# A memory-recurrent attention step: a postponed turning moves between the halves of P times V, a quarter of a filler unit moves behind the output products

## The chip, the cores and the metric

The kernel runs on one core of a Trainium2 chip. The metric is the device time of one execution in microseconds (us); several executions are measured and their median is given. The engines are called by the names of the profile: PE (matrix products; PEld are its weight loads), DVE, ACT and POOL (vector work and copies), SP (issues transfers). Each engine works through its own queue in the order in which the program was written.

## The reference

One block of a transformer, forward and backward, in bfloat16: sequence length 2048, model width 448. Attention runs over 64 segments of 32 tokens, one after the other; each segment is preceded by 8 memory tokens, which are the first 8 outputs of the segment before.

```
for s in range(n_seg):                       # 64 segments
    xs = x[:, s*32:(s+1)*32, :]
    h = concatenate([mem, xs], axis=1)       # 8 + 32 = 40 tokens
    q, k, v = h @ Wq, h @ Wk, h @ Wv         # 16 heads of 256
    p = softmax(where(mask, q @ k^T * scale, -1e9))
    o = (p @ v) @ Wo
    mem = o[:, :8, :]
    outs.append(o[:, 8:, :])
h  = x + A(layernorm(x));  h2 = h + swiglu_ffn(layernorm(h))
```

The outputs are h2 and the gradients with respect to the input, the first memory and all weights.

## The kernel before

The program has four stages: the forward chain over the 64 segments, the feed-forward part with its gradients, the backward chain over the segments, and a tail with the weight gradients. The change touches only the first, `forward_chain`. The order on every engine there is the order of the code: no scheduler moves anything.

A step `s` of the loop is one segment; four steps make one tile of 128 tokens (`t = s // 4`, `r = s % 4`). The step computes only what depends on the memory. A segment's window of 32 tokens in `hA` holds the 8 memory tokens and the first 24 tokens of the segment. The last 8 tokens of each segment do not become memory's input; for four segments together they make 32 rows of their own (`hB`), whose projections and output products are done in units that are spread over the steps as filler.

**Filler units.** `cur` is the unit of this step, `late` that of the step before. At r = 0 the unit is `o_units(t - 1)`: the output products of those 32 rows of the tile before. At r = 1, 2, 3 it is `b_units(t + 1, ...)` for k, q and v of the next tile. A unit has the parts u1 (first half of its columns), e1 (its copy out), u2 and u3 (two quarters, into one accumulator `p1`), e3 (the copy of `p1`), and, in a later step, ut (turning: PE transposes the result) and et (the copies of what was turned). For k and q, ut is 8 transposes and et two copies on ACT; for v both are empty; for `o_units`, u2 and u3 are 16 products of 224 columns each, e3 a copy on ACT into `partB`, ut two float32 transposes and et four small sums on DVE.

**A step, in order.** K and Q of the window (`proj`, line 545, 64 products), their turning (line 559), V (line 553), scores (line 590), softmax on DVE and ACT, u1 of the filler, the turning of P in two halves (`p_turn`, line 863) with copies by ACT for half 0 and by DVE for half 1 (`p_ev`), and u2 between them. Then P times V (line 897) in two halves, each of which makes two accumulators `po` (four in all). Each `po` is emptied by two copies: a large one into `oA` right away (DVE for `gg` = 0, ACT for `gg` = 1) and a small one into `oB`, collected in the list `obs` and issued after both halves. Between the halves stands `cur["u3"]()`. Then the output products (`wo_mm`, line 674, 64 of 224 columns) go into the accumulator `pO`, in the order in which the parts of `oA` become ready. DVE copies `pO` into `part`; `turn(part)` (line 598, two float32 transposes) and two sums on DVE (`gsum`, line 603) make the next segment's memory tokens in `hA`, with which the next step's projections start. While DVE copies `pO`, PE does `late["ut"]()`, and at r = 0 `prep_pe` (line 529: four transposes of the next tile's rows). `prep_ev` copies those (four copies on ACT, one on DVE) and `prep_load` fetches the rows of the tile after that on SP's queue. et follows one step later, at the head of the step, through `late2`.

**Accumulators.** All of them but the two for the scores come from the pool `psA` (`ps1`, line 499) with six buffers of 128 x 512 float32. A new accumulator gets a buffer whose last use in the code lies before the allocation; its first product waits until that use has ended.

Copies in this stage go through the helpers `V` (DVE, line 505), `A` (ACT, line 508) and `G_` (POOL, line 511), so all copies of an engine have one line in the profile; their shapes tell them apart: 128x256 are the large copies of `po`, 128x64 the small ones, 128x224 the copy of `pO`.

Of the kernel before, what the change touches and what calls it, by code (L numbers as in the profile page):

```python
# [265 lines left out]
def run_all(k: _K):  # L266
# [115 lines left out]
    with tc.manual_schedule():  # L382
# [86 lines left out]
        feed = ffn_phase(k, WT, ff, ffn, mv2, rstd2, {"o": Wo2, "v": Wv2, "k": Wk2, "q": Wq2}, back)  # L469
        k.feed = feed  # L470
        forward_chain(k, hA, NWIN, Wq_sb, Wk_sb, Wv_sb, Wo_sb, maskr, fwd, fwd, ff, feed)
        nc.gpsimd.dma_start(out=memTd[0:DB], in_=memT_all[0:DB].rearrange("p c s m -> p c (s m)"))
        next(feed)
# [7 lines left out]
def forward_chain(k: _K, hA, NWIN, Wq_sb, Wk_sb, Wv_sb, Wo_sb, maskr, work, stage, ff, feed):  # L481
    nc, tc = k.nc, k.tc
    S, D, M, H, Dh, HD = k.S, k.D, k.M, k.H, k.Dh, k.HD
    SEG, L, NSEG, NT, KC, DP, MC, DC = k.SEG, k.L, k.NSEG, k.NT, k.KC, k.DP, k.MC, k.DC
# [14 lines left out]
    def ps1(dtype=FP32):  # L499
        if dtype == FP32:  # L500
            return k.pspool.tile([P, 512], FP32, tag="ps", name="psf")
        return k.pspool.tile([P, 1024], BF16, tag="ps", name="psh")

    def V(out, in_):
        nc.vector.tensor_copy(out=out, in_=in_)  # L505

    def A(out, in_):
        nc.scalar.copy(out=out, in_=in_)  # L508
# [4 lines left out]
    def slot(s):  # L513
        return s % NWIN
# [3 lines left out]
    def fw(kc):  # L518
        return (kc % 2) * 2 * DB + (kc // 2) * DB

    def prep_load(t):
        xl = work.tile([P, DP], BF16, name="xload", tag="xload", bufs=1)
        nc.sync.dma_start(out=xl[:, 0:D], in_=dr["XN"][t * P:(t + 1) * P, :])
        return xl

    def prep_pe(xl):
        pt = ps1(BF16)
        for kc in range(KC):
            nc.tensor.transpose(pt[0:DB, kc * P:(kc + 1) * P], xl[:, fw(kc):fw(kc) + DB], ident[:, :])
        return pt  # L530

    def prep_ev(pt, t):
        v = pt[0:DB, 0:KC * P].rearrange("p (c r j) -> p c r j", c=KC, r=4)
        s0 = slot(4 * t)
        for r in range(4):
            A(hA[0:DB, :, s0 + r, M:SEG], v[:, :, r, 0:XA])
        hB = stage.tile([P, KC, 4, M], BF16, name="hB", tag="hB", bufs=2)
        V(hB[0:DB], v[:, :, :, XA:SEG])
        return hB
# [55 lines left out]
    def turn(src):  # L595
        y = ps1(FP32)
        for j in range(2):
            nc.tensor.transpose(y[0:DB, j * P:(j + 1) * P], src[:, j * DB:(j + 1) * DB], identf[:, :])
        return y[0:DB, 0:2 * P].rearrange("p (c b n) -> p c n b", c=KC, b=2)
# [13 lines left out]
    tiles = {}  # L613
# [63 lines left out]
    def o_units(t):  # L677
        T = tiles[t]
        st = {}

        def mm(i0, i1):
            for i in range(i0, i1):
                for c in range(4 * i, 4 * i + 4):
                    wo_mm(st["pO"], T.oB[:, c, :], c, c % 2, c < 2, c >= MC - 2)

        def u1():
            st["pO"] = ps1(FP32)
            mm(0, 4)

        def e1():  # L690
            pass

        def u2():
            mm(4, 6)

        def u3():
            mm(6, 8)

        def e3():
            A(partB[:, 0:2 * DB], st["pO"][:, 0:2 * DB])  # L700

        def ut():
            st["y"] = turn(partB)

        def et():
            for kc in range(KC):
                gsum(T.aT[0:DB, kc, :].rearrange("p (r j) -> p r j", r=4)[:, :, XA:SEG],
                     st["y"][:, kc, :, :].rearrange("p (r i) g -> p r i g", r=4))
        return dict(u1=u1, e1=e1, u2=u2, u3=u3, e3=e3, ut=ut, et=et)

    def none_units():
        def f():
            pass
        return dict(u1=f, e1=f, u2=f, u3=f, e3=f, ut=f, et=f)
# [18 lines left out]
    def v_b_rows(s, V_sb):  # L733
        t, r = divmod(s, 4)
        for g in range(G):
            gg, g2 = divmod(g, 2)
            eng = nc.gpsimd if s == 0 else nc.sync
            eng.dma_start(out=V_sb[QB * gg + SEG:QB * gg + L, g2 * GF:(g2 + 1) * GF],
                          in_=tiles[t].vB[32 * g + M * r:32 * g + M * (r + 1), :])
# [11 lines left out]
    xl = k.xl0  # L751
    tiles[0].hB = prep_ev(prep_pe(xl), 0)
    xl_next = k.rest_rows()
# [13 lines left out]
    mask_mm(0)  # L767
    mask_mm(1)
    late = none_units()
    late2 = none_units()  # L770

    for s in range(NSEG):
        t, r = divmod(s, 4)
        sl = slot(s)
        T = tiles[t]
        if r == 0:
# [7 lines left out]
            cur = o_units(t - 1) if t > 0 else none_units()  # L784
        else:
            cur = b_units(t + 1, "?kqv"[r]) if t + 1 < NT else none_units()
# [1 line left out]
        def stat(kc):  # L788
            return hA[0:DB, kc, sl, :]

        late2["et"]()
        kT = work.tile([P, MC, L], BF16, name="kT", bufs=1)
        qT = work.tile([P, MC, L], BF16, name="qT", bufs=1)
        nc.gpsimd.tensor_copy(out=kT[:, :, SEG:L], in_=T.kB[:, :, r * M:(r + 1) * M])
# [92 lines left out]
        obs = []  # L887
        for half in range(2):
            if half == 1:
                cur["u3"]()  # L890
            for gg in range(2):
                po = ps1()
                pw = po[:, 0:8 * L].rearrange("p (a e c n) -> p a e c n", a=2, e=2, c=DC)
                for i in range(2):
                    for dc in range(DC):
                        c0 = gg * GF + half * HB + i * Dh + dc * P
                        nc.tensor.matmul(pw[:, i, :, dc, :], lhsT=V_sb[0:NR, c0:c0 + P],
                                         rhs=PT[0:NR, half, 2 * gg + i, :].rearrange("p (e n) -> p e n", e=2),
                                         start=True, stop=True)
                pov = po[:, 0:8 * L].rearrange("p (g j n) -> p g j n", g=2, j=4)  # L900
                eng = V if gg == 0 else A
                eng(oAv[:, 2 * gg:2 * gg + 2, 4 * half:4 * half + 4, r * SEG:(r + 1) * SEG], pov[:, :, :, 0:SEG])
                obs.append((eng, oBv[:, 2 * gg:2 * gg + 2, 4 * half:4 * half + 4, r * M:(r + 1) * M], pov[:, :, :, SEG:L]))
        for eng, o_, i_ in obs:
            eng(o_, i_)
        if s == NSEG - 2:
            v_b_rows(s + 1, V_sb)
        if final:
# [6 lines left out]
            c = order[i]  # L915
            wo_mm(pO, T.oA[:, c, r * SEG:(r + 1) * SEG], c, i % 2, i < 2, i >= MC - 2)
        V(part[:, 0:2 * DB], pO[:, 0:2 * DB])
        late["ut"]()
        if final:
            uo = o_units(t)  # L920
            uo["u1"]()
            uo["u2"]()
            uo["u3"]()
            next(feed)
        if r == 0 and t + 1 < NT:
            xl = xl_next
            ppx = prep_pe(xl)
        y = turn(part)
        if r == 2 and t > 0:
            out_pe(t - 1)  # L930
# [5 lines left out]
        if s + 1 < NSEG:  # L936
            nc.gpsimd.tensor_copy(out=memT_all[0:DB, :, s + 1, :], in_=hA[0:DB, :, slot(s + 1), 0:M])
        cur["e3"]()
        if r == 0 and t + 1 < NT:
            tiles[t + 1].hB = prep_ev(ppx, t + 1)  # L940
            if t + 2 < NT:
                xl_next = prep_load(t + 2)
        if r == 2 and t > 0:
            out_ev(t - 1)
        if r == 3:
            nc.gpsimd.dma_start(out=dr["OTA"][t], in_=T.oA[:].rearrange("p c n -> p (c n)"))
            nc.gpsimd.dma_start(out=dr["OTB"][t], in_=T.oB[:].rearrange("p c n -> p (c n)"))
        late2 = late
        late = cur

    uo["e3"]()
# [1065 lines left out]
```

## Time and profile before

| what | us |
|---|---|
| median of 3 executions | 2963.6 |
| lowest and highest of them | 2957.69, 2975.01 |
| the profiled execution's own time | 2993.99 |
| its span, first to last instruction | 2992.2 |
| the forward steps in it, first to last product of P times V | about 79 to 970 |

The profiled execution took 1% longer than the median. In the page, slices 2 to 12 of 40 (each 74.8 us) are the forward steps, and PE is busy 9 tenths in nearly all of them:

```profile
PE   2999999999998799988999999999998999989988
...
PEclk8999999999999999998999999999998999999999
```

The first row is the busy share of PE in tenths, the second the clock granted to PE in tenths of full speed. Within the stage, the order of lines in one step repeats every 13.7 to 14.3 us; the timeline of such a step, with start and length of each group of instructions, tells which engine waits for which. In the timeline, "[0.17 <-PE psf L897]" is the idle time of that engine just before the row, and who ended it.

### The profile page before, as it was taken

What the parts mean: (1) busy time and instruction counts of PE and PEld (TensorE: products, weight loads), DVE (VectorE), ACT (ScalarE), POOL (GpSimd) and SP (SyncE); (2) the same over time, 40 slices, a digit from 0 to 9 for tenths busy, and PEclk for the clock granted to TensorE, in tenths of its full rate; (3) what the DMA queues carried; (4) which work ended last, traced back from release to release, by engine and by line L of the source; (5) the groups of instructions that cost most, each with busy time, mean ns of one, the idle gap of its engine ahead of it and who ended that gap; (6) DMA issues with size and microseconds to landing.
All of it is one profiled execution on the core that took longest, in us unless ns stands there. A gap on an engine that the chain in (4) does not pass through costs nothing.

```text
span 2992.2 us, 104631 instructions
## 1 busy us (share of the span) xinstructions
PE 2762.4 (92%) x44552; PEld 1526.9 (51%) x44588; DVE 1546.5 (52%) x4068; ACT 1173.8 (39%) x3032; POOL 740.3 (25%) x1388
## 2 busy tenths in 40 slices
PE   2999999999998799988999999999998999989988
PEld 1555555555554455544555555555554554434444
DVE  3666666666665577765555556666562111112221
ACT  1544544444444565654444444444442011101100
POOL 1222222222222122212222222322222223222231
PEclk8999999999999999998999999999998999999999
DMA  9344344344346853395556556655657999999996
GB/s 255 113 129 136 122 127 132 122 126 132 117 126 170 197 160 113 122 225 152 143 156 190 150 142 175 177 144 151 180 156 274 269 209 215 199 183 205 209 178 116
DMA packets 623393, 493.59 MB, mean 165 GB/s; under 512 B 486128, under 2 KB 535648, under 8 KB 613392
## 3 DMA queue, kind: packets, MB, share of 16 engines
q1 hardware_dynamic: 574592, 295.20, 45.2%
q0 software_dynamic: 48336, 191.70, 19.8%
q8 instruction: 352, 5.77, 0.8%
q14 instruction: 113, 0.93, 0.1%
HBM read 137.50 MB, written 221.94 MB: 120 GB/s over the span
## 4 chain that ended last, share of the span: by engine, by line
PE 44%; DVE 5%; issue 2%; DMA 2%; ACT 1%; SPq 1%; POOL 0%; POOLq 0%; DVEq 0%; ACTq 0%
PE psf L1860 13%; PE psf L1364 9%; PE psf L1336 4%; PE psf L1845 4%; PE psf L1666 3%; PE psf L1873 2%; PE s_ps L1364 2%; PE s_ps L1644 1%; PE psf L1371 1%; PE psh L1342 1%; PE psh L1693 1%; ACT arena L1330 1%; DVE arena L1654 1%; DVE arena L1648 1%; DVE arena L1651 1%
## 5 line engine op out<-in xcount | busy, mean ns | idle before, releaser
L1860 PE MATMUL psf<-wall,arena 128*128 128x512 bf16 (+1 forms) x1788 | 394.1, 375 | 15.7 <-DMA wall<-dKA 12.9
L508 ACT CAST arena<-psf 128x512 bf16<-128x512 f32 (+2 forms) x560 | 236.3, 454 | 367.8 <-PE psf L545 257.2
L1364 PE MATMUL psf<-wall,arena 128*32 128x448 bf16 x6144 | 340.3, 362 | 16.4 <-issue 10.6
L545 PE MATMUL psf<-wall,arena 112*32 112x512 bf16 x5120 | 308.4, 383 | 38.4 <-DMA wall<-in_A_Wk_dram 20.3
L1330 ACT CAST arena<-psf 128x256 bf16<-128x256 f32 (+1 forms) x597 | 234.9, 421 | 262.4 <-PE psf L1336 184.8
L1860 PEld LDWEIGHTS <-arena 128*128 128x128 bf16 x1824 | 176.4, 98 | 215.5 <-issue 23.9
L1775 DVE CAST arena<-psf 128x512 bf16<-128x512 f32 (+1 forms) x75 | 49.7, 662 | 435.1 <-PE psf L1860 285.8
L505 DVE CAST arena<-psf 128x512 bf16<-128x512 f32 (+2 forms) x432 | 191.8, 469 | 129.9 <-PE psf L545 91.2
L1773 ACT CAST arena<-psf 128x448 bf16<-128x448 f32 (+1 forms) x83 | 46.5, 560 | 500.3 <-PE psf L1860 293.8
L1364 PEld LDWEIGHTS <-arena 128*32 128x32 bf16 x6144 | 155.3, 98 | 137.9 <-issue 34.0
L545 PEld LDWEIGHTS <-arena 112*32 112x32 bf16 x5120 | 126.3, 97 | 168.8 <-issue 34.7
L1327 DVE CAST arena<-psf 128x256 bf16<-128x256 f32 (+1 forms) x339 | 164.8, 486 | 80.0 <-PE psf L1666 47.0
L1845 PE MATMUL psf<-arena,wall 128*128 128x448 bf16 x864 | 172.3, 358 | 21.0 <-DMA wall<-OTA 14.5
L553 PE MATMUL psf<-wall,arena 112*32 112x512 bf16 x2560 | 169.2, 385 | 12.5 <-DMA wall<-in_A_Wv_dram 12.5
L1336 PE MATMUL psf<-wall,arena 128*32 128x512 bf16 x2560 | 162.1, 383 | 15.6 <-DVE arena L1376 15.3
L508 ACT COPY arena<-psh 40x160 bf16<-40x160 bf16 (+2 forms) x320 | 119.4, 401 | 95.1 <-PE psh L657 53.8
L1666 PE MATMUL psf<-arena 40*128 40x40 bf16 x6144 | 147.3, 178 | 8.6 <-issue 3.9
L674 PE MATMUL psf<-wall,arena 128*32 128x224 bf16 x5120 | 149.2, 267 | 0.6 <-issue 0.6
L1719 POOL COPY arena<-arena 128x32 bf16<-128x32 bf16 x63 | 13.3, 211 | 548.9 <-DVE arena L1376 548.9
L1666 PEld LDWEIGHTS <-arena 40*128 40x128 bf16 x6144 | 126.3, 93 | 39.6 <-issue 19.0
L511 POOL COPY arena<-arena 32x512 bf16<-32x512 bf16 x129 | 78.2, 606 | 267.0 <-ACT arena L508 263.2
L1845 PEld LDWEIGHTS <-wall 128*128 128x128 bf16 x864 | 84.5, 99 | 100.5 <-DMA wall<-OTA 17.3
(222 smaller groups left out, 4487.6 us busy)
## 6 DMA issues: line engine op xcount, KB each, us to landing
Vtok<-arena SPq DMA_DIRECT2D x128, 192.0 KB
KtokA<-arena SPq DMA_DIRECT2D x64, 256.0 KB
QtokA<-arena SPq DMA_DIRECT2D x64, 256.0 KB
OTA<-arena POOLq DMA_DIRECT2D x16, 1024.0 KB, 5.1
arena<-QtokA SPq DMA_DIRECT2D x128, 128.0 KB
arena<-KtokA SPq DMA_DIRECT2D x128, 128.0 KB
dVA<-arena POOLq DMA_DIRECT2D x16, 1024.0 KB, 5.2
dKA<-arena POOLq DMA_DIRECT2D x16, 1024.0 KB, 7.4
```

The source lines that it names most:

```text
L505: nc.vector.tensor_copy(out=out, in_=in_)
L508: nc.scalar.copy(out=out, in_=in_)
L545: nc.tensor.matmul(ps[32 * g:32 * g + 32, :], lhsT=stat(kc), rhs=W_sb[0:DB, kc, c0:c0 + HB], start=(kc == 0), stop=(kc == KC - 1))
L553: nc.tensor.matmul(ps[32 * g:32 * g + 32, :].rearrange("t (y d) -> t y d", y=2), lhsT=stat(kc), rhs=wv[:, x, :, half, e, :], start=(kc == ...
L674: nc.tensor.matmul(ps[32 * g:32 * g + 32, 0:2 * DB], lhsT=x, rhs=Wo_sb[:, c, a * 2 * DB:(a + 1) * 2 * DB], start=first, stop=last)
L1327: nc.vector.tensor_copy(out=out, in_=in_)
L1330: nc.scalar.copy(out=out, in_=in_)
L1336: nc.tensor.matmul(ps[32 * g:32 * g + 32, :], lhsT=stat(kc), rhs=WoT_sb[:, kc, c0:c0 + HB], start=(kc == 0), stop=(kc == KC - 1))
L1364: nc.tensor.matmul(pO[32 * g:32 * g + 32, 0:D], lhsT=ch(c), rhs=WT[:, c, :], start=(first and i < 4), stop=(last and i >= MC - 4), skip_gr ...
L1666: nc.tensor.matmul(po[:, n * L:(n + 1) * L], lhsT=lhs[b:b + L, lc:lc + P], rhs=rhs[b:b + L, hh, 0:L], start=True, stop=True)
L1845: nc.tensor.matmul(ps[:, 0:D], lhsT=stat[:, i, c * P:(c + 1) * P], rhs=Y[:, i, 0:D], start=(i == 0), stop=(i == kts - 1))
L1860: nc.tensor.matmul(ps[:, 0:N], lhsT=Hx[:, i, dc * P:(dc + 1) * P], rhs=X[:, i, b * N:(b + 1) * N], start=(i == 0), stop=(i == kts - 1))
```

## The change

In the loop over the segments:

- between the halves of P times V, `late["ut"]()` and, at r = 0, `prep_pe` take the place of `cur["u3"]()`;
- `cur["u3"]()` goes behind the output products and DVE's copy of `pO`, where `late["ut"]()` and `prep_pe` stood;
- `late["et"]()`, and at r = 0 `prep_ev` and `prep_load`, follow right after the small copies `obs`, in the same step as the turning; `late2` goes.

```diff
     late = none_units()
-    late2 = none_units()
...
-        late2["et"]()
         kT = work.tile([P, MC, L], BF16, name="kT", bufs=1)
...
         for half in range(2):
             if half == 1:
-                cur["u3"]()
+                late["ut"]()
+                if r == 0 and t + 1 < NT:
+                    ppx = prep_pe(xl_next)
             for gg in range(2):
...
         for eng, o_, i_ in obs:
             eng(o_, i_)
+        late["et"]()
+        if r == 0 and t + 1 < NT:
+            tiles[t + 1].hB = prep_ev(ppx, t + 1)
+            if t + 2 < NT:
+                xl_next = prep_load(t + 2)
...
         V(part[:, 0:2 * DB], pO[:, 0:2 * DB])
-        late["ut"]()
+        cur["u3"]()
...
-        if r == 0 and t + 1 < NT:
-            xl = xl_next
-            ppx = prep_pe(xl)
         y = turn(part)
...
         cur["e3"]()
-        if r == 0 and t + 1 < NT:
-            tiles[t + 1].hB = prep_ev(ppx, t + 1)
-            if t + 2 < NT:
-                xl_next = prep_load(t + 2)
...
-        late2 = late
         late = cur
```

## The prediction

> **What bounds the kernel now.** I read the page first, then the busy time by stretch, then the timeline of one step, then single copies, then the granted clock around stalls.
>
> ```profile
> span 2992.2 us, 104631 instructions
> PE 2762.4 (92%) x44552; PEld 1526.9 (51%) x44588; DVE 1546.5 (52%) x4068; ACT 1173.8 (39%) x3032; POOL 740.3 (25%) x1388
> ```
>
> TensorE (PE) is busy 92% of the whole. The change touches the forward steps alone, so I took the stretch from 106 to 906 us, which holds steps 2 to 59 (columns: busy time and count of PE, weight loads, DVE, ACT, POOL, then granted clock, DMA share, GB/s):
>
> ```profile
> 106.00:906.00 800.00, 774.40 (x16057) 448.23 (x16050) 523.83 (x1651) 389.46 (x978) 194.71 (x415) 1.00 0.41 127
> ```
>
> PE is busy 774.4 of 800 us at full clock. So 25.6 us is all the idle PE time that any reordering of these 58 steps could win (0.44 us a step), while whatever makes PE wait is paid in full. The last third of step 19 (r = 3), from the timeline (start, length, engine, line):
>
> ```profile
> 344.06 0.53 PE L897 MATMUL psf<-arena 104*128 104x80 bf16 x8
> 344.40 0.49 DVE L505 COPY arena<-psh 40x160 bf16<-40x160 bf16 x2
> 344.53 0.61 PE L553 MATMUL psf<-wall,arena 112*32 112x512 bf16 x8
> ...
> 345.08 0.46 PE L897 MATMUL psf<-arena 104*128 104x80 bf16 x8
> 345.46 1.46 PEld L674 LDWEIGHTS <-arena 128*32 128x32 bf16 x64
> 345.47 1.72 PE L674 MATMUL psf<-wall,arena 128*32 128x224 bf16 x64
> 345.57 0.61 ACT L508 CAST arena<-psf 128x256 bf16<-128x256 f32 x3 [0.17 <-PE psf L897]
> 347.11 0.45 PEld L657 LDWEIGHTS <-arena 128*128 128x128 bf16 x8 [0.18 <-issue]
> 347.12 0.62 PE L657 MATMUL psh<-ident,arena 128*128 128x128 bf16 x8
> 347.24 0.39 DVE L505 COPY arena<-psf 128x224 f32<-128x224 f32 x1 [1.12 <-PE psf L674]
> 347.68 0.43 PE L598 MATMUL psf<-identf,arena 128*112 128x128 f32 x2
> ...
> 348.22 0.49 DVE L603 TENSOR_REDUCE arena<-psf 112x32 bf16<-112x64 f32 x2 [0.59 <-PE psf L598]
> ```
>
> L897 is P times V (two halves), L553 between them is u3, L674 the 64 output products (Wo), L657 the postponed turning, L598 turn(part). PE goes from the second half straight into Wo at 345.47, while ACT is still emptying that half (345.57 to 346.18). Behind Wo a serial chain closes the step: copy of pO on DVE, turn(part), the sum L603, the next step's projections. The turning fills the 0.56 us (347.12 to 347.68) in which PE would otherwise wait for the copy.
>
> **The change part by part.** No arithmetic is removed; instructions change places.
>
> (1) *Filler swapped between the halves.* u3 (8 products of 512 columns, 344.53 to 345.08: 0.55 us) leaves; in r = 2, 3 the 8 turnings come. Sixteen turnings of the same form at L559 run from 310.20 to 311.29, 1.09 us, so 8 take 0.55: no difference. In r = 1 two float32 turnings come (about 0.43 us by L598), in r = 0 four turnings (0.43 us at L529) replace 16 products of 224 columns (302.71 to 303.21: 0.50). Shorter filler only helps until half 1 waits for DVE's P copies: at r = 0 they end at 302.55 + 0.49 = 303.04, half 1 starts at 303.21, so with 0.06 for the hand-over 0.10 is won; at r = 1 316.84 against 316.96, 0.06, of which ACT, busy without a break there (1.58 us from 316.49), lets about 0.03 through to what follows.
>
> (2) *u3 behind Wo.* 0.55 us (0.50 at r = 0) in a hole of 0.56: nothing. The cover is DVE's copy of pO; without it 0.55 a step would be bare. I keep 0 to +0.05 a step (0 to 3 us) for the range.
>
> (3) *The copies in the same step.* Two ACT copies of 0.59 us (r = 2, 3), four ACT copies (0.66) and one DVE copy (0.21) at r = 0, four small DVE sums (0.61) at r = 1. ACT is idle from 346.18 until 347.77 and needed again some 4 us later; DVE idles 1.12 us before the copy of pO, and 0.61 fits. Cost 0. The load of the next rows moves forward on SP's queue but stays between the Vtok stores and the next L738 loads; on POOL's queue only the K and Q stores hang on e3, which keeps its place. Cost 0.
>
> (4) *An added wait.* This is what decides. The pool psA has six buffers. When pO is allocated before, five are held: u2's p1 (emptied by e3 only after turn(part)) and four products po (emptied by the postponed small copies `obs`). The sixth is free. After, the turning's result sits in that sixth until its copies, so pO must take a buffer of po. In the built program the first Wo product of steps 2 to 59 waits for ACT's small copy (128x64) out of the second po and takes that buffer; before, it waited only for copies that lie earlier. Steps 0, 1 and 60 to 63, in which a unit or the turning is missing, do not have the wait. ACT's order is: large copy of the last po, small copy of the second, and so on. The window that ends inside the small copy shows these two:
>
> ```profile
> 345.57 0.49 ACT L508 CAST arena<-psf 128x256 bf16<-128x256 f32 x2 [0.17 <-PE psf L897]
> ```
>
> They end at 345.57 + 0.49 = 346.06. The hand-over from DVE to PE is 0.05 (the copy of pO ends at 347.63, turn(part) starts at 347.68); for ACT I take the same, with 0 and 0.10 as ends. So Wo starts at 346.11 instead of 345.47: 0.64, say 0.65 us, with nothing on PE to fill it, because u3, the turn, the masks and the next projections stand behind Wo in PE's queue, and DVE (copy of pO), ACT and POOL wait for them in turn. The large copy cannot come earlier: it waits for the last product of half 1.
>
> **The sum.** r = 2, 3: 30 steps x 0.65 = 19.5; r = 0: 14 x (0.65 - 0.10) = 7.7; r = 1: 14 x (0.65 - 0.03) = 8.7; together 36 us.
>
> To that comes the clock, in a small way. The stretch already has stalls in front of P times V (8.6 us over 16 waits for DMA and ACT, 0.54 each), and they lie in the 2 us before the new hole. Three stretches (columns as above):
>
> ```profile
> 779.90:783.10 3.20, 3.20 (x71) 2.58 (x64) 0.62 (x4) 0.55 (x3) 0.00 (x0) 0.59 0.42 119
> 775.70:779.10 3.40, 2.29 (x33) 0.88 (x29) 2.43 (x9) 2.42 (x6) 0.55 (x1) 1.00 0.45 139
> 581.10:584.50 3.40, 2.29 (x76) 1.90 (x78) 1.84 (x7) 1.64 (x6) 0.47 (x1) 1.00 0.72 233
> ```
>
> With 1.11 us idle in 3.4, the clock fell right behind one stretch (0.59; Wo took 3.05 there instead of 1.72, so 1.3 us lost) and not behind the other. A step with a stall of 0.54 and a hole of 0.65 has 1.2. If a quarter of the 16 pay 1.3, that is 5; I take 4 us, with 0 and 16 x 1.3 = 21 as ends.
>
> Sum +40 us: the profiled span of 2992.2 would become 3032. The shown median is 2963.6 (2957.7 to 2975.0), 1% below that execution; the steps do not depend on it, so I add the same 40: **3004 us**.
>
> The Trainium skill, "TensorE: Matmul & The Clock Gate", section "A second HAM failure mode: psum-queue depth-cycling", says that a PE which idles briefly between groups because accumulator banks cycle can swing between half and full clock; it speaks against this change, since a hole in every step is what it describes. By it the sum would be the clock rival's below; the trace so far agrees only in part, for 1.11 us idle made the clock fall once and once not.
>
> **The rivals.**
> *The clock falls in every step.* The hole of 0.65 plus about 0.1 of old idle is 0.75 in 3.4 us. The stretches from 523.1 and 721.1 have 0.8 and 0.77 idle at clock 1.00 and nothing falls behind them, which speaks against; the holes being regular speaks for. Price 58 x 1.3 = 75 on top of 36: 3075 us.
> *Not slower: the hole pays for itself.* If pO's buffer came free before half 1 ends, part (4) would be nothing and (1) stays: 14 x 0.10 + 14 x 0.03 = 1.8 us won, and at the very most all of the 25.6 idle. About 2955 us with a third of it. It decides only if Wo's first product does not follow ACT's small copy; against it is that this copy stands behind a large copy which itself waits for half 1.
> *The change does nothing that counts.* Stalls that DMA causes shrink by what the hole adds, because loads gain 0.65 us a step. That could absorb 8.6 us of 36 at most, not all; 2965 to 2975 us would need the hole to be under 0.2 us.
>
> **How the numbers follow.** The forecast gets 0.87, the clock rival 0.07, no effect 0.03, the gain 0.03. Range: low end 58 x 0.55 (hand-over 0, 0.05 won everywhere) = 32, less 8.6 of shrunken stalls and 4 for the median's own scatter, +19: 2983. High end 58 x 0.70 = 41, +3 from (2), +21 clock, +3 scatter: +68, cut to +64 as they hardly meet: 3028. What a measurement can tell from no change is about 0.5%, 15 us. Faster 0.03, same 0.03, slower 0.94.
>
> **What would show it.** In the changed profile: Wo (L674) starting about 1.04 us after the first product of half 1 instead of 0.39 (345.08 to 345.47), with ACT's L508 as releaser, a new idle of 35 to 40 us over the forward stage; L657 between the halves without shifting half 1; u3 behind Wo with turn(part) still 0.56 after Wo; granted clock 1.00 in most stretches. If Wo follows half 1 without a gap, or a step like step 17 (L545 from 306.63 to 320.38) stays at 13.75 us, the reasoning is wrong. If the steps are 0.65 longer and the total far over 3028, it is the clock.

## The result and the profile after

| | before | after |
|---|---|---|
| median, us | 2964.59 (6 executions, 2957.69 to 2975.01) | 3004.85 (6 executions, 2998.91 to 3024.26) |
| profiled execution, its own time / span, us | 2993.99 / 2992.2 | 3004.55 / 3002.8 |
| first product of P times V in step 2 to that in step 60 (58 steps), us | 810.5 | 840.6 |

The changed kernel is slower: ratio 1.0128, 95% interval 1.0094 to 1.0163, that is 28 to 48 us; the medians differ by 40. The forecast was 3004.

The page of the changed kernel, span and busy time of the engines:

```profile
span 3002.8 us, 104689 instructions
PE 2751.8 (92%) x44552; PEld 1536.1 (51%) x44588; DVE 1546.4 (51%) x4068; ACT 1168.9 (39%) x3032; POOL 738.0 (25%) x1388
```

PE executes the same 44552 products and is busy 10 us less over the whole; the spans differ by only 10.6 us although the forward stage alone grew by 30. The rest of the execution (span less the 58 steps) was 2181.7 us before and 2162.2 after, and between 2138.5 and 2170.1 in the experiments: it scatters by more than the effect. Mechanisms are therefore read from the stage, and the whole times serve for the verdict. Each kernel has one profile, so a difference of a few us between two stages can be scatter too.

The same 58 steps in both kernels by busy time (columns: window, its length, busy time and count of PE, weight loads, DVE, ACT, POOL, then granted clock, DMA share, GB/s). Before:

```profile
108.00:918.00 810.00, 784.11 (x16281) 454.56 (x16280) 529.23 (x1665) 393.50 (x987) 198.19 (x423) 1.00 0.41 128
```

After:

```profile
101.00:941.00 840.00, 780.30 (x16278) 464.64 (x16277) 529.91 (x1663) 388.70 (x985) 197.21 (x422) 1.00 0.40 123
```

PE's idle time is 810.00 - 784.11 = 25.9 us before and 840.00 - 780.30 = 59.7 after: 33.8 more, at full clock both times. What PE waited for in these windows (total us, times, longest), largest first. Before:

```profile
PE psf L897 <- DMA arena<-arena: 4.6, 9, 1.1
PE psf L897 <- ACT arena L508: 4.0, 7, 1.0
```

After:

```profile
PE psf L674 <- ACT arena L508: 19.0, 33, 0.6
PE psf L674 <- DVE arena L505: 14.3, 25, 0.6
PE psf L897 <- DMA arena<-arena: 3.9, 12, 0.8
PE psf L897 <- DVE arena L505: 2.6, 12, 0.7
```

A wait in front of Wo (L674), absent before, stands in front of all 58 (33 + 25) and makes 33.3 of the 33.8 us. The view names ACT in 33 steps and DVE in 25. Which of the two it is can be read from single rows, here of step 19, the step that the prediction showed of before (r = 3). Timeline of after:

```profile
347.98 0.30 PE L897 MATMUL psf<-arena 104*128 104x80 bf16 x4 [0.21 <-PE psh L861]
...
348.60 0.61 PE L657 MATMUL psh<-ident,arena 128*128 128x128 bf16 x8
...
349.10 0.45 PE L897 MATMUL psf<-arena 104*128 104x80 bf16 x8
349.44 0.69 DVE L505 CAST arena<-psf 128x256 bf16<-128x256 f32 x3 [0.38 <-PE psf L897]
...
349.58 0.60 ACT L508 CAST arena<-psf 128x256 bf16<-128x256 f32 x3 [0.41 <-PE psf L897]
350.06 1.11 ACT L508 COPY arena<-psh 128x512 bf16<-128x512 bf16 x2
350.12 1.72 PE L674 MATMUL psf<-wall,arena 128*32 128x224 bf16 x64 [0.57 <-DVE arena L505]
...
351.65 0.62 PE L553 MATMUL psf<-wall,arena 112*32 112x512 bf16 x8
351.88 0.39 DVE L505 COPY arena<-psf 128x224 f32<-128x224 f32 x1 [1.76 <-PE psf L674]
...
352.33 0.43 PE L598 MATMUL psf<-identf,arena 128*112 128x128 f32 x2
```

The turning (L657) is between the halves, u3 (L553) behind Wo. PE is done with half 1 at 349.55 and then stands still for 0.57 us. ACT's group (its large copy, the small copy of the second `po`, that of the fourth) begins at 349.58; its second member, the small copy in question, ends at 349.85 + 0.22 = 350.07, and Wo starts 0.05 later. DVE's two small copies of `po` end at 350.00 and 350.13, 0.12 before the start of Wo and just behind it. Over all 58 steps the distance from the end of that ACT copy to the start of Wo is 0.050 to 0.052 us, also where the view names DVE, while the distance from either small copy of DVE varies by 0.09. That is the wait which part (4) of the prediction named.

### The profile page after: what moved, and what is told of

Read it like the earlier page. It is cut to its first block, busy times and chain, and to the rows that moved or that the text cites. A ratio compares the mean times of both kernels' runs of the same rounds, so it can differ in the third digit from the quotient of the medians.

```text
span 3002.8 us, 104689 instructions
## 1 busy us (share of the span) xinstructions
PE 2751.8 (92%) x44552; PEld 1536.1 (51%) x44588; DVE 1546.4 (51%) x4068; ACT 1168.9 (39%) x3032; POOL 738.0 (25%) x1388
## 4 chain that ended last, share of the span: by engine, by line
PE 43%; DVE 5%; issue 2%; DMA 2%; ACT 1%; SPq 1%; POOL 0%; POOLq 0%; DVEq 0%; ACTq 0%
PE psf L1857 13%; PE psf L1361 9%; PE psf L1333 4%; PE psf L1842 4%; PE psf L1663 3%; PE psf L1870 2%; PE s_ps L1361 1%; PE s_ps L1641 1%; PE psf L1368 1%; PE psh L1339 1%; PE psh L1690 1%; DVE arena L1651 1%; DVE arena L1645 1%; DVE arena L1648 1%; DVE rsum L1647 1%
## 5 line engine op out<-in xcount | busy, mean ns | idle before, releaser
L1361 PE MATMUL psf<-wall,arena 128*32 128x448 bf16 x6144 | 332.7, 357 | 12.7 <-issue 6.7
L1361 PEld LDWEIGHTS <-arena 128*32 128x32 bf16 x6144 | 153.6, 97 | 129.6 <-issue 23.2
L674 PE MATMUL psf<-wall,arena 128*32 128x224 bf16 x5120 | 149.2, 270 | 33.3 <-ACT arena L508 19.0
L553 PE MATMUL psf<-wall,arena 112*32 112x512 bf16 x2560 | 169.3, 384 | 10.3 <-DMA wall<-in_A_Wv_dram 10.3
L674 PEld LDWEIGHTS <-arena 128*32 128x32 bf16 x5120 | 129.9, 101 | 43.0 <-issue 31.6
L1039 ACT COPY wall<-psh 128x896 bf16<-128x896 bf16 (+1 forms) x142 | 105.0, 832 | 77.1 <-PE psh L1127 46.3
```

What stands on the lines that cost most here:

```text
L553: nc.tensor.matmul(ps[32 * g:32 * g + 32, :].rearrange("t (y d) -> t y d", y=2), lhsT=stat(kc), rhs=wv[:, x, :, half, e, :], start=(kc == ...
L674: nc.tensor.matmul(ps[32 * g:32 * g + 32, 0:2 * DB], lhsT=x, rhs=Wo_sb[:, c, a * 2 * DB:(a + 1) * 2 * DB], start=first, stop=last)
L1361: nc.tensor.matmul(pO[32 * g:32 * g + 32, 0:D], lhsT=ch(c), rhs=WT[:, c, :], start=(first and i < 4), stop=(last and i >= MC - 4), skip_gr ...
```

## The experiments

All comparisons are with executions of the kernel before in the same session: median 2971.66 (19 executions) for the first four below, 2978.43 (20) for the last three. "Stage" is the length of the 58 steps in the profiled execution, 810.5 us before.

**1. The wait without the moves.** The kernel before, in which `pO` is given the accumulator of the second `po`; no instruction changes its place.

```diff
-        obs = []
+        obs, pos = [], []
...
+                pos.append(po)
...
-        pO = ps1()
+        pO = pos[1]
```

> The kernel before, every instruction in its old place, but pO is written into the buffer of the second po (the one that ACT empties), so that the wait of the changed kernel is there without its moves. Theory: a hole of 0.6-0.65 us ahead of Wo in all 64 steps, 64 x 0.64 = 41 less some 8 of shrunken stalls: 2993-3008 us, ratio 1.010-1.015, about the time of the changed kernel. Rival (places of the filler): 2965 us, ratio 1.000.

Measured: median 3017.98 (4 executions), ratio 1.0144 [1.0066, 1.0221]; stage 855.8, +45.3. The waits view of this kernel:

```profile
PE psf L674 <- DVE arena L505: 31.0, 54, 0.6
```

and one of its steps (r = 2), half 1 and Wo:

```profile
345.47 0.46 PE L898 MATMUL psf<-arena 104*128 104x80 bf16 x8
346.50 1.72 PE L674 MATMUL psf<-wall,arena 128*32 128x224 bf16 x64 [0.57 <-DVE arena L505]
```

The same wait of 0.57 us, in the old order, makes the kernel at least as slow as the change does; the time is above the 2993 to 3008 that was expected. The moves are not needed for the loss. Of the 45 us, 36.8 are the longer way from half 1 to Wo (median 1.04 us from start to start, 0.39 before). Another 4.1 come from a turn(part) that starts some 0.06 later in each step, because DVE's copy of `pO` does; 2.5 lie in Wo, with two more half-clock stretches, and 1.6 between the halves. Why the copy of `pO` starts later was not tried.

**2. The moves without the wait.** After, but `pO` is put where no other accumulator lives: the second half of the columns of a score accumulator. The products of Wo then carry the flag `skip_group_check`, as those of the scores do.

```diff
-                             start=first, stop=last)
+                             start=first, stop=last, skip_group_check=skip)
...
-        pO = ps1()
+        pO = k.fix[0][:, 256:512]
```

> The changed kernel, but pO lies in columns 256 to 480 of the first score accumulator, which are not used by the scores, and takes no buffer of the pool. Theory: no wait is left, Wo follows half 1 at once (0.39 us after half 1's first product, as before), the small gains at r = 0 and 1 remain (1.8 us): 2958-2968 us, ratio 0.998-1.001. Rival (places of filler and copies): 3000-3010 us, ratio 1.012.

Measured: median 2979.29 (10), ratio 1.0027 [0.9994, 1.0060]; stage 809.6, -0.9. Its waits view:

```profile
PE psf L598 <- DVE arena L505: 9.6, 57, 0.2
PE psf L897 <- DMA arena<-arena: 5.2, 15, 0.9
```

No wait at L674 is left, and the stage is as long as before. The time lies above the expected 2958 to 2968, but its interval holds "no change". turn(part) (L598) now begins 0.06 us later in most steps. Since the other place of `pO` might itself cost or gain, its control is number 6.

**3. The wait shortened at its source.** After, with the small copies of half 0 issued at the end of half 0 instead of behind both halves. The moves stay, and so does the shared buffer.

```diff
+            if half == 0:
+                for eng, o_, i_ in obs:
+                    eng(o_, i_)
+                obs = []
```

> The changed kernel, but the two small copies of half 0 (obs) are issued right behind half 0's large copies, ahead of half 1's. Theory (pO must wait for the buffer of a po): the buffer comes free while half 1 still runs, Wo starts within 0.1 us of where it did before the change (0.25 at r = 1, where ACT is busy without a break), so the hole of 0.65 shrinks to 0.0-0.25 us and the time falls to 2964-2972 us, ratio to before 1.000-1.003. Rival (the new places of u3, of the turning or of its copies cost the time): 3000-3010 us, ratio 1.012. Rival clock: granted clock of the stage as in the changed kernel, time in between.

Measured: median 2971.39 (10), ratio 1.0006 [0.9975, 1.0037]; stage 814.5, +4.0. Step 22 (r = 2) in its timeline:

```profile
377.32 0.61 PE L657 MATMUL psh<-ident,arena 128*128 128x128 bf16 x8
377.90 0.53 PE L897 MATMUL psf<-arena 104*128 104x80 bf16 x8
378.48 1.72 PE L674 MATMUL psf<-wall,arena 128*32 128x224 bf16 x64
```

Wo follows 0.58 us behind the start of half 1, without an idle time in front of it; in after it is 1.11 in most steps. Counted from the first product of P times V it is 1.53 us, in number 2 1.41, so a little of the wait is left. The late small copy, and not the sharing of the buffer as such, is the cost.

**4. The wait made longer.** After, with the copies of the turned unit (et) ahead of the small copies, and `pO` in the second `po` as before.

```diff
+        late["et"]()
         for eng, o_, i_ in obs:
             eng(o_, i_)
-        late["et"]()
...
-        pO = ps1()
+        pO = pos[1]
```

> The changed kernel with pO fixed in the buffer of the second po and the copies of the turned result (et) ahead of the small copies, so that at r = 2 and 3 the awaited small copy stands behind two more ACT copies. They add 2 x 0.48 = 0.97 us to the hole in 30 steps, 29 us, and the 5 steps that had no wait get one, 3 us. Theory: 3005 + 32 = 3037 us, ratio 1.024, if the clock stays. If holes of 1.6 us make the clock fall for 3.4 us behind each of those 30 steps at 1.3 us a time: 3037 + 39 = 3076 us, with granted clock near 0.9 in the stage. Rival (places): 3005 us, as the copies have no reader that is due.

Measured: median 3067.86 (4), ratio 1.0299 [1.0240, 1.0357]; stage 894.8, +84.3. At r = 2, 3 ACT now does two copies of 128x512 first, and Wo starts 2.08 us behind the start of half 1. Two stretches of this kernel with such a wait, each followed by the stretch behind it (columns as above):

```profile
421.70:425.10 3.40, 1.45 (x32) 1.40 (x36) 1.88 (x7) 2.90 (x8) 0.49 (x1) 1.00 0.84 233
425.10:428.50 3.40, 3.40 (x72) 2.78 (x64) 0.39 (x1) 0.00 (x0) 0.00 (x0) 0.51 0.24 81
592.40:595.80 3.40, 1.84 (x63) 1.73 (x65) 1.07 (x5) 2.09 (x7) 0.00 (x0) 1.00 0.90 260
595.80:599.20 3.40, 3.27 (x70) 1.77 (x65) 2.16 (x6) 0.00 (x0) 0.42 (x2) 1.00 0.06 23
```

With 1.95 us idle of 3.4 the granted clock fell to half in the next stretch; with 1.56 it did not, here. In all there are 14 half-clock stretches in this stage, against one before. Added up over the 58 steps, the way from the first product of P times V to Wo grew by 61.6 us, Wo itself, which the half clock hits first, by 15.2, and the way from there to the next projections by 7.6, together the 84. So the loss grows with the delay of this one copy, and the clock comes in only when the wait is long.

**5. u3 behind Wo alone.** The kernel before, with u3 behind Wo and the turning, and nothing between the halves: the cover of the prediction's part (2), used twice.

```diff
-            if half == 1:
-                cur["u3"]()
...
+        cur["u3"]()
```

> The kernel before with u3 alone moved behind Wo, behind the postponed turning, which stays there; nothing stands between the halves. No buffer is missing, so no wait ahead of Wo. The filler behind Wo is now longer than the 0.56 us that DVE's copy covers: r = 2, 3: 0.48 + 0.55 - 0.56 = +0.47 a step; r = 1: 0.35; r = 0: 0.21; half 1 starts as soon as the P copies are there, 0.13 earlier at r = 2, 3, 0.10 at r = 0, 0.03 at r = 1. Sum 30 x 0.34 + 14 x 0.11 + 14 x 0.32 = 16 us: 2980-2992 us, ratio 1.005, by time that PE works in the chain and not by a hole ahead of Wo. Rival (u3 behind Wo is what the change costs): as slow as the changed kernel, 1.012 or more.

Measured: median 2987.64 (10), ratio 1.0034 [1.0004, 1.0065]; stage 827.2, +16.7. Two views of it, the waits and the end of a step with r = 3:

```profile
PE psf L895 <- DVE arena L505: 13.8, 36, 0.5
```

```profile
397.76 0.62 PE L657 MATMUL psh<-ident,arena 128*128 128x128 bf16 x8
398.31 0.62 PE L553 MATMUL psf<-wall,arena 112*32 112x512 bf16 x8
398.86 0.43 PE L598 MATMUL psf<-identf,arena 128*112 128x128 f32 x2
```

Two fillers of 0.55 us stand in a hole that fits one; the second delays turn(part) (median way from the start of the last product of Wo to the next P times V 11.42 us at r = 2, 3, 10.89 before). Between the halves PE now waits for the copies of P. In the median step nothing comes back there (1.40 us from the first product of P times V to Wo, as before); but where half 0 has to wait, half 1 now follows it sooner, and summed over the 58 steps this way is 11 us shorter. u3 behind Wo is free only because the turning has left.

**6. The other place of `pO`, without the moves.** The kernel before with the change of number 2.

> The kernel before with pO in the unused columns of the first score accumulator, the control for the same edit in the changed kernel. Theory: no wait was there to be taken away, the time stays: ratio 0.998-1.003 (up to 58 x 0.07 = 4 us more if turn(part) gets one more semaphore to look at, as it did there). If it is faster by 10 us or more, the six buffers already cost something before the change.

Measured: median 2987.33 (10), ratio 1.0035 [1.0007, 1.0062]; stage 815.9, +5.4. The place itself costs a little, and the ratio lies just above what was expected. Number 2 has the same place and the moves, and its ratio is 1.0027: the moves without the wait cost nothing that these runs can show. In the whole times they gain nothing either, but the stage of number 2 is 6.3 us shorter than this one. That gain lies between the first product of P times V and Wo: 80.3 us over the 58 steps there, 87.6 here.

**7. The swap without the earlier et.** After, with et one step later through `late2`, as before. The copies of `prep_ev` at r = 0 keep the place that they have in after.

```diff
+        late2["et"]()
...
-        late["et"]()
...
+        late2 = late
```

> The changed kernel without its third part: the copies of the turned result (et) stay at the head of the next step but one, as before; only the filler is swapped. Theory: the turned result still holds the sixth buffer, pO still takes that of the second po, the hole of 0.65 stays: ratio 1.009-1.016, 3000-3015 us. Rival (the copies in the same step cost the time): ratio 1.000.

Measured: median 3004.16 (5), ratio 1.0091 [1.0047, 1.0136]; stage 842.9, +32.4. Its waits:

```profile
PE psf L674 <- DVE arena L505: 20.1, 35, 0.6
PE psf L674 <- ACT arena L508: 12.7, 22, 0.6
```

The wait is there (32.8 us) although et's copies did not move. What decides is which accumulators are held when `pO` is allocated, and that the swap alone sets. That et now follows in the same step neither causes nor cures the wait.

## Why the prediction was right, point by point

**The wait (4): right in place, cause and size.** Wo was to start 1.04 us behind the first product of half 1, released by ACT's small copy: in step 19 it is 349.10 to 350.12, 1.02. Counted from the first product of P times V, the median way to Wo grew from 1.40 to 2.05 us at r = 1, 2, 3 (+0.65) and from 1.40 to 1.97 at r = 0 (+0.57). Over 44 and 14 steps that is 36.6 us against the forecast's 36; in number 1, with the old order, the way from half 1 to Wo alone grew by 36.8. Number 1 shows the wait alone doing it, 2 and 3 that without it no loss that the times can show remains.

**The swap between the halves (1): right in sign, too small.** In the median step at r = 1, 2, 3 it gains nothing: half 1 starts 0.07 us earlier but then lasts 0.53 instead of 0.46, and its end, which the copies in front of Wo follow, stays where it was. Summed over the 58 steps it gains more than the 1.8 us of the prediction. With u3 between the halves the way from the first product of P times V to Wo takes 86.2 us (before) and 87.6 (number 6), with the turning there 80.3 (number 2); with the wait it takes 124.7 (number 1) against 118.3 (after) and 118.5 (number 7). That is 6 to 7 us. Part of it lies in the steps whose half 0 had to wait (12 before, 8 in after): in after the median way is 1.85 us in these and 2.05 in all, with u3 between the halves it is 1.40 in both (before). The prediction read its gain from steps without such a stall. Where the rest lies was not followed.

**u3 behind Wo (2) and the copies (3): nothing, as said.** From the start of the last product of Wo to the next P times V it is 10.88 us after and 10.89 before at r = 1, 2, 3. Number 5 gives the bare price of the cover when it is used twice.

**The clock: mis-sized.** The sum took 4 us. There are two half-clock stretches in after's 58 steps and one before, which is 1.3 us more. The rival with a falling clock in every step, 3075 us, did not come; number 4 shows that its mechanism exists, at waits of 1.6 us. By the Trainium skill, "TensorE: Matmul & The Clock Gate", section "A second HAM failure mode: psum-queue depth-cycling", short idle gaps while accumulator banks cycle can make the clock swing. The trace of after does not agree for a gap of 0.57 us in every step (granted clock 1.00 over the stage, with the two half-clock stretches in it); the trace of number 4 does for 1.6 us, in less than half of its 30 steps with that wait.

**The stage: 30 us, not 40.** The sum was 36 for the wait less the swap and 4 for the clock. From start to start, the +30.1 us of after divide into +32.0 from the first product of P times V to Wo, +1.3 in Wo and -3.2 from the next projections to the next P times V; the way between Wo and the projections is the same. So the wait cost what was said; the swap gave back 6 us instead of 1.8, and the clock took 1.3 instead of 4. The -3.2 are waits right in front of half 0 (5.8 us before, 2.5 in after), which the sum left out and for which the range kept 8.6. That the wait makes them shrink is not shown: in numbers 1 and 7, with the same wait, the same way grew by 0.2 and 1.8.

**The whole.** That the medians differ by 40, like the forecast, is partly luck: the stage gave 30, and the interval of 28 to 48 holds both. What lies outside the stage is, but for six steps, not touched by the change, and its scatter (2138 to 2182 us) hides ten microseconds easily.

## What to carry to other kernels

Before moving work past an allocation, count the accumulators that are held there: the moved result keeps one, and the next allocation takes a buffer whose last reader may be the least urgent copy of all, as it was here. A wait that ends right behind a small copy is then cured by issuing that copy earlier (number 3). Where an effect of 1% sits in one stage, compare the lengths of that stage in the profiles, since the scatter of the rest can be as large as the effect, and compare sums beside medians: what the swap gained shows in no median step.

## What the runs showed of the hardware

The granted clock tolerated a wait of 0.57 us in every step of 14.5 us but for two falls, and it fell to half for 3.4 us behind most, not all, of the stretches in which PE was idle 1.55 us or more of 3.4 us (number 4: 12 of 19, in stretches of 3.41 us laid end to end from the falls). Below that it fell seldom, and not by the idle time alone. In after it fell behind the first of these two stretches, with 0.96 us idle, and not behind the second, with 1.18 (columns as above):

```profile
301.20:304.60 3.40, 2.44 (x56) 1.61 (x46) 3.17 (x12) 2.50 (x9) 0.56 (x1) 1.00 0.43 134
331.90:335.30 3.40, 2.22 (x36) 1.46 (x35) 2.63 (x11) 2.61 (x8) 0.55 (x1) 1.00 0.47 147
```

The least idle time behind which it fell in any of these runs is 0.82 us (number 4).

With `pO` in the other half of a score accumulator, turn(part) starts 0.15 us behind the end of DVE's copy of `pO` instead of 0.05, and about 0.06 us later in the step (numbers 2 and 6). Its cause was not tried.
